# Batch 0 of a pooled attention with gated feed-forward: v pooled in two halves of the heads, with the order and the banks of the first values changed

## The chip, the cores and the metric

The kernel runs on one core of a Trainium2 chip. A core has TensorE (PE, matmuls; PEld is its weight load), VectorE (DVE), ScalarE (ACT), GpSimd (POOL) and SyncE (SP, which here only issues DMAs). Matmuls write to PSUM, eight banks of 512 fp32 columns on 128 partitions. The metric is the device time in microseconds (us) from launch to end.

## The reference

Inputs are q, k, v of shape (8 batches, 8 heads, 576 positions, 64) and two weights, 512x2048 and 2048x512. The output has 4608 rows (8 x 576) of 512.

```
k_p = k.reshape(B, H, 72, 8, 64).mean(axis=3)         # v_p in the same way
scores = q @ k_p^T / 8
attn = softmax(scores)                                # over 72 pooled keys
x = (attn @ v_p), heads side by side                  # 4608 x 512
h = x @ w_in                                          # "up"
out = (h * cos(h)) @ w_out                            # "down"
```

## The kernel before, in words

The 4608 rows of x are held transposed in `xT` and worked off in nine tiles of 512 rows. For each tile t the "up" matmul (`up_mm`, L347) makes h in eight pairs of 128 columns of d_ff, each over four chunks of the contraction (128 rows of `xT` each, two heads); `up_g` (L357) takes the cosine on ACT and multiplies on DVE. Then the "down" matmul makes the output rows, and among its matmuls stands the attention of the next batch. From tile 1 on, down is done in seven products of halved matrices instead of eight.

The order of the work on each engine is the order of the source (`manual_schedule`): each engine works off its instructions in the order in which the code issues them, and waits stand where a tile is read or written. So within PE nothing overtakes.

Ahead of tile 0 stands the attention of batch 0 alone (L533 to L559), since no other work is there to fill the gaps. It is in four units `us[0]` to `us[3]`: units 0 and 1 are heads 0 to 3 at positions 0 to 255 and 256 to 511, units 2 and 3 the same positions of heads 4 to 7. Each unit passes these steps:

- `scores` (L222): eight matmuls or less into a pair of banks, and the exponential on ACT (L240), which leaves `ex`.
- `sums_first` (L306): four matmuls of `ex` with ones (L312), whose logarithm (L316) and exponential of its negative (L317) on ACT give the inverse of the softmax sum. Logarithm and exponential stand in one table of ACT; the sine for up needs another, loaded once by `sin_tables` (L334).
- `values_then` (L320): four matmuls of `ex` with the pooled v (L326) and a DVE multiply by the inverse into `xT` (L328).

Units 0 and 1 fill chunks 0 and 1 of `xT`, units 2 and 3 chunks 2 and 3. So `up_mm(0, 0, 0, 2)` and `up_mm(0, 1, 0, 2)`, the first halves of the contraction of the first two pairs, need units 0 and 1 alone (four matmuls each), and the second halves, which begin tile 0 in the loop (L568), need all four units.

v is pooled on PE by `pool_v_mm` (L181): nine steps, each with a matmul for either half of the partitions (L185), add the groups of eight rows into the two halves of the pair of banks `banks[1]`, 256 columns (four head pairs of 64) in each; one DVE copy (L187) brings all of it to `vz`.

PSUM is three pairs of banks, `banks[0]` to `banks[2]`, and two single banks, `obanks[0]` and `obanks[1]`. The up matmul of tile 0 uses `banks[0]`, `banks[1]`, `banks[2]` in turn. The inverses lie in three buffers in turn (`p1_sb`, `v_sb`, `q_sb`), so that unit 3's takes the buffer of unit 0's.

Batch 0's v is the fourth of the loads on the POOL queue (L490); its landing is what pooling waits for.

Of the kernel before, what the change touches and what calls it, by code (L numbers as in the profile page):

```python
# [20 lines left out]
def kernel(  # L21
# [9 lines left out]
    nc = tc.nc  # L31
    B, H, S, D = q.shape
    Sp = S // POOL
# [4 lines left out]
    KCH = d_model // 128  # L38
# [45 lines left out]
    banks = [psum.tile([128, 2, 512], FP32, name=f"bank{i}") for i in range(3)]  # L84
    obanks = [psum.tile([128, 512], FP32, name=f"obank{i}") for i in range(2)]
# [51 lines left out]
    def v_part(b):  # L137
        return vz[b % 2][:, :, 0:4:3, :]
# [39 lines left out]
                                     start=(t == 0), stop=(t == ROW - 1))  # L178
        return lambda copy: put_kk(b, ps, pj0, pj1, copy)

    def pool_v_mm(b, pair):  # L181
        vb = staged["v", b]
        for t in range(ROW):
            for hp, rows in enumerate(half):
                nc.tensor.matmul(pair[:Sp, hp, 0:KCH * D], lhsT=groups[rows, t, :], rhs=vb[rows, :, t, :],  # L185
                                 start=(t == 0), stop=(t == ROW - 1))
        nc.vector.tensor_copy(out=v_part(b).rearrange("p j a d -> p a j d"),  # L187
                              in_=pair[:Sp, :, 0:KCH * D].rearrange("p a (j d) -> p a j d", j=KCH))

    def k_transpose(b):  # L190
        for i in range(2):
# [25 lines left out]
    def ex_col(u, i):  # L217

        (c0, n), (h0, nh) = u
        return (i // 2 % 2 * (nh // 2) + i // 4 * 2 + i % 2) * n  # L220

    def scores(b, u, pair):  # L222
        scores_mm(b, u, pair)
        scores_exp(b, u, pair)
# [19 lines left out]
    def x_out(b, u, rows):  # L244
        (c0, n), (h0, nh) = u
        return xT[rows, h0 // 2:(h0 + nh) // 2, b * S + c0:b * S + c0 + n]

    def cols(x, u):
        n = u[0][1]
        return x[:, 0:n * u[1][1] // 2].rearrange("p (j n) -> p j n", n=n)  # L250
# [3 lines left out]
    def inverse_tile(w):  # L254

        if early_inverses:
            name = early_inverses.pop(0)
            return msb.tile([128, 2, 256], FP32, name=name, tag=name, bufs=1).rearrange("p a m -> p (a m)")[:, 0:w]
        inv = asb.tile([128, 512], FP32, name="inv", tag="inv", bufs=1)
        return inv[:, 0:w]  # L260
# [45 lines left out]
    def sums_first(b, u, cs):  # L306

        (c0, n), (h0, nh) = u
        ex = att["ex", b, u]
        for i in range(nh):  # L310
            hp = i % 2
            nc.tensor.matmul(cs[hp * 64:hp * 64 + 64, (i // 2) * n:(i // 2 + 1) * n], lhsT=ones[:Sp, :],  # L312
                             rhs=ex[:, ex_col(u, i):ex_col(u, i) + n])
        w = nh * n // 2
        inv = inverse_tile(w)
        nc.scalar.activation(out=inv, in_=cs[:, 0:w], func=ACTF.Ln)  # L316
        nc.scalar.activation(out=inv, in_=inv, func=ACTF.Exp, scale=-1.0)  # L317
        att["inv", b, u] = inv

    def values_then(b, u, ao):  # L320

        (c0, n), (h0, nh) = u
        ex = att.pop(("ex", b, u))
        for i in range(nh):
            pj, hp = divmod(h0 + i, 2)
            nc.tensor.matmul(ao[hp * 64:hp * 64 + 64, (i // 2) * n:(i // 2 + 1) * n],  # L326
                             lhsT=vz[b % 2][:, pj, 3 * hp, :], rhs=ex[:, ex_col(u, i):ex_col(u, i) + n])
        nc.vector.tensor_mul(out=x_out(b, u, slice(0, 128)), in0=cols(ao, u), in1=cols(att.pop(("inv", b, u)), u))  # L328
# [12 lines left out]
    def up_bank(t, fp):  # L341
        i = list(up_order(t)).index(fp)
        if t < FIRST:
            return banks[i % 3]
        return (banks[0], banks[2], banks[1], obanks)[i % 4 if i < 7 else 0]

    def up_mm(t, fp, k0=0, k1=KCH):  # L347

        h = up_bank(t, fp)
        for j in range(2):  # L350
            fc = 2 * fp + j
            for ki in range(k0, k1):
                nc.tensor.matmul(h[j] if h is obanks else h[:, j, :], lhsT=w_in_sb[fc // 4][:, ki, (fc % 4) * 128:(fc % 4 + 1) * 128],  # L353
                                 rhs=xT[:, ki, t * TILE:(t + 1) * TILE],
                                 start=(ki == 0), stop=(ki == KCH - 1))
# [139 lines left out]
    groups = g3.rearrange("p f n -> p (f n)")[:, 0:ROW * Sp].rearrange("p (t n) -> p t n", t=ROW)  # L495
# [34 lines left out]
    us = BY_HEADS  # L530
# [16 lines left out]
    warm_up(2, banks[1][:, 0, :])  # L547
    scores(0, us[2], banks[0])
    scores(0, us[3], banks[2])
    pool_v_mm(0, banks[1])  # L550
    sums_first(0, us[2], obanks[0])
    values_then(0, us[0], obanks[1])
    values_then(0, us[1], banks[1][:, 0, :])
    sums_first(0, us[3], banks[2][:, 0, :])
    values_then(0, us[2], obanks[1])
    values_then(0, us[3], obanks[0])
    up_mm(0, 0, 0, 2)
    up_mm(0, 1, 0, 2)
    sin_tables()  # L559

    for t in range(NT):
        b = t + 1
# [50 lines left out]
        if t == 0:  # L613
            fill = [(2, fill[0][1]), (2, S_(0, 0)), (8, lambda: pool_v_mm(1, banks[1])),
                    (8, lambda: values(t, REST, banks[2])), (8, S_(1, 0)), (8, V_(0, 1)),
                    (18, S_(2, 2)), (21, V_(1, 0, later)), (26, S_(3, 1)), (32, lambda: later.pop()()),
                    (32, V_(2, 2)), (40, V_(3, 0))]
# [132 lines left out]
```

The softmax here doesn't subtract the row's maximum and nothing guards it: scores larger than these inputs give would overflow.

## Time and profile before

| | |
|---|---|
| median of 6 runs | 286.06 us (285.85 to 286.32) |
| the profiled execution | 286.57 us, its span 284.8 us |
| PE | 274.7 us busy, 96% |
| DVE | 215.3 us, 76% |
| ACT | 164.3 us, 58% |
| POOL | 143.3 us, 50% |
| granted TensorE clock | 1.000 over the span |
| v of batch 0 has landed, pooling starts | 12.96 us |
| first up matmul of tile 0 | 16.83 us |

Times within the profile are microseconds from the span's start. A row of the timeline is start, length, engine, line, operation, what is written and read, shape and count; in brackets stands how long the engine had been idle before it and who ended that. A matmul's length is from its start to its modelled end; as matmuls are pipelined, the distance between two starts is what a matmul costs, and rows that stand for several matmuls reach from the first start to the last end. In the chain of work that ended last, each line is a start, a length and a piece of work, and the piece above it is what it waited for.

### The profile page before, as it was taken

The numbers are of one execution on the slowest core, as the hardware profiler recorded it, in microseconds if no ns is written. First come the engines' busy times: TensorE is split into PE (matmuls) and PEld (weight loads), VectorE is DVE, ScalarE is ACT, GpSimd is POOL, SyncE is SP. The second block draws the span as 40 slices with busy tenths as digits, with TensorE's granted clock in tenths as the row PEclk, the third lists the DMA queues.
The fourth block names the chain that finished last, engine by engine and source line by source line (L and its number), as shares of the span: only waits on it lengthen the run. The fifth ranks groups of instructions, "written<-read, shape, count | busy, mean of one in ns | idle before, by whom it ended". The sixth has DMA issues, their size and how long they took to land.

```text
span 284.8 us, 5835 instructions
## 1 busy us (share of the span) xinstructions
PE 274.7 (96%) x2338; PEld 176.4 (62%) x2360; DVE 215.3 (76%) x314; ACT 164.3 (58%) x193; POOL 143.3 (50%) x150
## 2 busy tenths in 40 slices
PE   7889999999999999999999999999999999999994
PEld 2645554446864586458745884588458844874583
DVE  5458747899958995699569956995699569856972
ACT  3886798367157735674566556655656555436600
POOL 8553079996698269924993499439900000000000
PEclk9999999999999999999999999999999999999999
DMA  7999999894949799997778868882660261015014
GB/s 160 199 206 207 207 204 218 124 186 68 137 47 112 148 213 175 139 172 151 111 135 155 175 97 150 147 175 57 123 148 3 55 130 38 0 24 125 2 37 111
DMA packets 57737, 36.12 MB, mean 127 GB/s; under 512 B 35440, under 2 KB 53360, under 8 KB 57712
## 3 DMA queue, kind: packets, MB, share of 16 engines
q0 software_dynamic: 19744, 18.07, 41.4%
q1 hardware_dynamic: 37328, 17.18, 30.9%
q10 hardware_dynamic: 640, 0.52, 0.8%
q8 instruction: 18, 0.29, 0.4%
q14 instruction: 7, 0.06, 0.1%
HBM read 36.70 MB, written 9.44 MB: 162 GB/s over the span
## 4 chain that ended last, share of the span: by engine, by line
PE 78%; DVE 10%; DMA 4%; ACT 3%; issue 1%; SPq 1%; DVEq 0%; ACTq 0%
PE bank L353 33%; PE obank L431 28%; PE obank L370 4%; DVE g_sb L367 4%; PE obank L353 4%; DMA out_dram<-o_two 3%; PE bank L233 3%; DVE g L397 2%; PE bank L431 2%; PE bank L295 2%; ACT cos L363 2%; PE bank L268 1%; SPq L467 1%; DVE w L387 1%; DMA g_sb<-in_k_dram 1%
## 5 line engine op out<-in xcount | busy, mean ns | idle before, releaser
L353 PE MATMUL bank<-xT,w_in_sb 128*128 128x512 bf16 x495 | 113.1, 379 | 1.1 <-DVE g_sb L367 0.2
L363 ACT ACTIVATE cos<-bank,half_pi 128x1024 f32<-128x1024 f32 x64 | 70.3, 1113 | 57.5 <-PE bank L353 55.6
L353 PEld LDWEIGHTS <-w_in_sb 128*128 128x128 bf16 x576 | 56.0, 98 | 66.3 <-issue 0.9
L367 DVE TENSOR_TENSOR g_sb<-bank,cos 128x1024 bf16<-128x1024 f32 x64 | 77.2, 1220 | 25.4 <-ACT cos L363 25.3
L156 POOL TENSOR_TENSOR half_sums<-kv_st 72x512 f32<-72x512 bf16 x48 | 54.7, 1167 | 0.6 <-issue 0.2
L240 ACT ACTIVATE ex<-bank 72x1024 bf16<-72x1024 f32 (+1 forms) x40 | 35.0, 928 | 34.0 <-PE bank L233 33.8
L431 PEld LDWEIGHTS <-g 128*128 128x128 bf16 x512 | 47.8, 98 | 6.2 <-issue 0.3
L431 PE MATMUL obank<-w,g 128*128 128x256 bf16 x368 | 42.7, 273 | 0.2 <-DVE p_sb L445 0.2
L431 PEld LDWEIGHTS <-g_sb 128*128 128x128 bf16 x384 | 36.7, 98 | 7.5 <-issue 0.5
L162 POOL TENSOR_TENSOR half_sums<-half_sums 72x512 f32<-72x512 f32 x24 | 30.4, 1288 | 0.0
L431 PE MATMUL obank<-w_out_sb,g_sb 128*128 128x256 bf16 x240 | 28.9, 273 | 0.0
L397 DVE TENSOR_TENSOR g<-g_sb 128x1024 bf16<-128x1024 bf16 x32 | 23.4, 730 | 0.5
L714 POOL COPY gate<-g 1x1 bf16<-1x1 bf16 x5 | 0.9, 180 | 33.3 <-DVE g L397 33.3
L300 DVE TENSOR_TENSOR x_rows<-bank,inv_rows 128x512 bf16<-128x512 f32 x24 | 16.6, 692 | 0.8
L431 PE MATMUL obank<-w,g_sb 128*128 128x256 bf16 x128 | 15.3, 273 | 0.4 <-DVE o_two L447 0.4
L431 PE MATMUL obank<-w_out_sb,g 128*128 128x256 bf16 x112 | 15.6, 273 | 0.0
L279 DVE TENSOR_TENSOR xT<-bank,inv 64x256 bf16<-64x256 f32 x14 | 5.9, 422 | 12.7 <-ACT inv L275 12.6
L353 PE MATMUL obank<-xT,w_in_sb 128*128 128x512 bf16 x64 | 15.1, 379 | 0.0
L370 PE MATMUL obank<-w_out_sb,g_sb 128*128 128x512 bf16 x61 | 14.7, 380 | 0.4 <-issue 0.3
L233 PE MATMUL bank<-qT,kk 64*72 64x128 bf16 (+2 forms) x288 | 12.6, 222 | 0.1
L233 PEld LDWEIGHTS <-kk 64*72 64x72 bf16 x288 | 9.0, 111 | 5.2 <-issue 3.6
L331 ACT ACT_TABLE_LOAD x9 | 11.5, 1283 | 0.9 <-PEq L734 0.7
(103 smaller groups left out, 276.3 us busy)
## 6 DMA issues: line engine op xcount, KB each, us to landing
out_dram<-o_two SPq DMA_DIRECT2D x64, 128.0 KB, 2.4
kv_st<-in_v_dram POOLq DMA_DIRECT2D x8, 576.0 KB, 11.5
kv_st<-in_k_dram POOLq DMA_DIRECT2D x7, 576.0 KB, 10.0
q_b<-in_q_dram POOLq DMA_DIRECT2D x6, 576.0 KB, 7.5
w_in_sb<-in_moe_w_in_dram POOLq DMA_DIRECT2D x4, 512.0 KB, 13.2
w_out_sb<-in_moe_w_out_dram POOLq DMA_DIRECT2D x4, 512.0 KB, 18.5
q_b<-in_q_dram POOLq DMA_DIRECT2D x4, 288.0 KB, 12.0
g_sb<-in_k_dram SPq DMA_DIRECT2D x1, 576.0 KB, 3.7
```

The costliest lines, as they stand in the source:

```text
L156: nc.gpsimd.tensor_tensor(out=s[:, h:h + 2], in0=x[:, h:h + 2, 0:4, :], in1=x[:, h:h + 2, 4:8, :], op=ADD)
L162: add(out=s[:, h:h + 4, 0:2, :], in0=s[:, h:h + 4, 0:2, :], in1=s[:, h:h + 4, 2:4, :], op=ADD)
L233: nc.tensor.matmul(pair[:Sp, bank, c:c + n].rearrange("p (g n) -> p g n", n=64), lhsT=kk[b % 2][half[r], key_slot(b, h0 + i, r), 0:Sp], rh ...
L240: nc.scalar.activation(out=ex[:, 0:nh * n].rearrange("p (a n) -> p a n", a=2), in_=pair[:Sp, :, 0:nh * n // 2], func=ACTF.Exp, scale=scale ...
L300: nc.vector.tensor_tensor(out=x[0:n].rearrange("p (j a d) -> p j a d", j=KCH, a=2), in0=ps[0:n, :, 0:2 * (D + 2)].rearrange("p j (a w) -> ...
L331: nc.scalar.preload_act_table_set("natural_log_exp_and_others")
L353: nc.tensor.matmul(h[j] if h is obanks else h[:, j, :], lhsT=w_in_sb[fc // 4][:, ki, (fc % 4) * 128:(fc % 4 + 1) * 128], rhs=xT[:, ki, t * ...
L363: nc.scalar.activation(out=c, in_=ps, func=ACTF.Sin, bias=half_pi[:, :1])
L367: nc.vector.tensor_mul(out=o, in0=ps, in1=c)
L370: nc.tensor.matmul(o, lhsT=g_sb[:, fc, ms * 128:(ms + 1) * 128], rhs=w_out_sb[fc // 4][:, fc % 4, :], start=(fc == 0), stop=(fc == FFCH - 1))
L397: nc.vector.tensor_tensor(out=out[:, f0:f1], in0=x, in1=y, op=op)
L431: mms.append(lambda bank=bank, first=first, g=g, w=w, fc=fc, p=p: nc.tensor.matmul(bank[p], lhsT=g(fc, p), rhs=w(fc), start=(first and fc ...
```

## The change

`pool_v_mm` takes a range of head pairs. For batch 0 it is called twice, for head pairs 0 and 1 (heads 0 to 3) and 2 and 3 (heads 4 to 7), each with 18 matmuls of 128 columns and a copy of half the size; both use the same columns of `banks[1]`, so that the second half's matmuls come after the first copy. The values of units 0 and 1 need the first half alone. The order on PE becomes: first half, values of unit 0, second half, values of unit 1, sums of unit 2, values of unit 2, sums of unit 3, the first up matmuls of pair 0, values of unit 3, the first up matmuls of pair 1. The values of unit 1 go to `obanks[0]` instead of `banks[1]`, the sums of unit 2 to `banks[0]` instead of `obanks[0]`. The order on DVE becomes: first copy, multiply of unit 0, second copy, multiplies of units 1, 2 and 3. ACT's order stays. For batch 1 the function is called as before, and no DMA is touched.

```diff
-    def pool_v_mm(b, pair):
+    def pool_v_mm(b, pair, j0=0, j1=KCH):
         vb = staged["v", b]
         for t in range(ROW):
             for hp, rows in enumerate(half):
-                nc.tensor.matmul(pair[:Sp, hp, 0:KCH * D], lhsT=groups[rows, t, :], rhs=vb[rows, :, t, :],
+                nc.tensor.matmul(pair[:Sp, hp, 0:(j1 - j0) * D], lhsT=groups[rows, t, :], rhs=vb[rows, j0:j1, t, :],
                                  start=(t == 0), stop=(t == ROW - 1))
-        nc.vector.tensor_copy(out=v_part(b).rearrange("p j a d -> p a j d"),
-                              in_=pair[:Sp, :, 0:KCH * D].rearrange("p a (j d) -> p a j d", j=KCH))
+        nc.vector.tensor_copy(out=v_part(b)[:, j0:j1].rearrange("p j a d -> p a j d"),
+                              in_=pair[:Sp, :, 0:(j1 - j0) * D].rearrange("p a (j d) -> p a j d", d=D))
...
-    pool_v_mm(0, banks[1])
-    sums_first(0, us[2], obanks[0])
+    pool_v_mm(0, banks[1], 0, 2)
     values_then(0, us[0], obanks[1])
-    values_then(0, us[1], banks[1][:, 0, :])
+    pool_v_mm(0, banks[1], 2, 4)
+    values_then(0, us[1], obanks[0])
+    sums_first(0, us[2], banks[0][:, 0, :])
+    values_then(0, us[2], obanks[1])
     sums_first(0, us[3], banks[2][:, 0, :])
-    values_then(0, us[2], obanks[1])
+    up_mm(0, 0, 0, 2)
     values_then(0, us[3], obanks[0])
-    up_mm(0, 0, 0, 2)
     up_mm(0, 1, 0, 2)
```

## The prediction

> **What bounds the kernel now.** I read the page first: TensorE (PE) is busy 274.7 of 284.8 us at a granted clock of nine tenths or more in every slice, and the chain that ended last is 78% PE. So PE sets the end, and the change can only matter through the moment from which PE runs without a break. That moment lies in the first 20 us. Next I read the chain there, in order of time (start, length, what).
>
> ```profile
> 13.02 1.01 ACT ex L240
> ...
> 14.22 0.70 DVE vz L187
> ...
> 14.96 0.43 PE obank L326 x4
> ...
> 15.49 0.70 DVE xT L328
> ...
> 16.23 0.63 PE obank L326 x8
> 16.86 0.35 PE bank L353
> ...
> 17.26 6.88 PE bank L353 x31
> ```
>
> Seen here: the copy of the pooled v (L187) leads to the first values (L326), one multiply and the other values, and from 16.86 on there is nothing but the up matmul. I read on to the end of this chain: later waits (a DVE stretch from 52 to 60 us, a store before 109.5 us) follow from PE's own progress, and only 0.4 us of PE idling there hangs on a store. So what the first 19 us lose or gain should reach the end nearly whole.
>
> The chain shows what was last, not what was nearly last. The up matmul has a second input gate: its second half of the contraction (k chunks 2 and 3) needs the products of units 2 and 3. Those pass through ScalarE (ACT), whose rows I read from the timeline (start, length).
>
> ```profile
> 14.83 0.59 ACT L316 ACTIVATE q_sb<-obank 128x512 f32<-128x512 f32 x1
> 15.45 0.63 ACT L317 ACTIVATE q_sb<-q_sb 128x512 f32<-128x512 f32 x1
> 16.27 0.60 ACT L316 ACTIVATE p_sb<-bank 128x512 f32<-128x512 f32 x1 [0.20 <-DVE xT L328]
> 16.90 0.63 ACT L317 ACTIVATE p_sb<-p_sb 128x512 f32<-128x512 f32 x1
> 17.55 1.28 ACT L334 ACT_TABLE_LOAD   x1
> ```
>
> Two logarithms (L316) and two exponentials (L317), the inverses of units 2 and 3, end at 17.53. The last multiply follows, on VectorE (DVE):
>
> ```profile
> 14.22 0.69 DVE L187 CAST vz<-bank 72x512 bf16<-72x512 f32 x1 [2.29 <-ACT ex L240]
> ...
> 17.56 0.69 DVE L328 TENSOR_TENSOR xT<-obank,p_sb 128x512 bf16<-128x512 f32 x1
> ```
>
> It ends at 18.25. PE, which began the up matmul at 16.83 at 0.2155 us each (17.47, 17.69, 17.90 in the timeline), comes to the ninth matmul, the first that needs this product, at 16.83 + 8 x 0.2155 = 18.55. With 0.05 us from a DVE end to a PE start (14.91 to 14.96) the gate stands only 18.55 - 18.30 = **0.25 us** from deciding.
>
> **The change, step by step.** Times are us from the span's start.
>
> *Pooling v, first half.* It starts at 12.96 as before, released by the landing of v.
>
> ```profile
> 12.96 1.17 PE L185 MATMUL bank<-kv_st,g 64*72 64x256 bf16 x18 [0.32 <-DMA kv_st<-in_v_dram]
> 14.07 0.41 PE L312 MATMUL obank<-ex,ones 72*64 72x256 bf16 x4
> ```
>
> Eighteen matmuls (nine pairs, the two row halves beside each other) move 128 columns instead of 256. No row has this form. The nearest:
>
> ```profile
> 9.01 0.77 PE L177 MATMUL obank<-g,kv_st 64*64 64x72 bf16 x36
> 10.31 0.45 PE L214 MATMUL bank<-identity,q_b 128*128 128x128 bf16 x5
> ```
>
> The five transposes of 128 columns start 0.056 apart in the trace, the pairs of 72 columns 0.033, the pairs of 256 columns 0.109. I take 0.056, the row with the same columns. It can't be below 0.054, half of the 256-column pace, since half the columns pass; nor does the weight load hold it up much, as the score matmuls with the same 64x72 weights (L233, 64 columns) go at 0.035. I allow up to 0.065. Last start 12.96 + 0.05 + 8 x 0.056 = 13.46, end 0.22 later (a 128-column row's length): **13.67** instead of 14.13.
>
> *First copy.* It starts 0.09 after (14.13 to 14.22). Length by two rows, 144 and 512 columns:
>
> ```profile
> L150 DVE CAST kk<-obank 64x144 bf16<-64x144 f32 x8 | 2.4, 304 | 3.3 <-PE obank L177 3.2
> ```
>
> (686 - 304) / 368 = 1.04 ns a column, so 256 columns take 0.42 (0.34 if all of 0.69 were halved, 0.47 at most, as neighbours with 256 columns are near 0.42). It ends at 13.76 + 0.42 = **14.18** instead of 14.91.
>
> *Values of unit 0* then start at 14.23 (14.96), 0.73 sooner; the second pair of matmuls starts at 14.37.
>
> *Pooling v, second half*, stands behind them on PE. Going over from one shape of matmul to another costs something, seen here:
>
> ```profile
> 35.70 1.17 PE L185 MATMUL bank<-kv_st,g 64*72 64x256 bf16 x18 [0.15 <-DVE g_sb L367]
> 36.80 0.41 PE L268 MATMUL bank<-ex,vz 72*128 72x64 bf16 x8
> ```
>
> The last pair starts at 36.60 in the trace and would let the next go at 36.71; it goes at 36.80, so 0.09 more. The second half starts at 14.37 + 0.20 = 14.57, its last pair at 15.07.
>
> *Values of unit 1* (the first half of v is enough for them) follow over another change of shape at 15.07 + 0.06 + 0.09 = 15.22, second pair 15.35. The second copy on DVE, behind the multiply of unit 0, ends about 15.79; nobody on this path waits for it.
>
> *Sums of unit 2.* This is the step that decides. Before, they ran at 14.07, in the time in which PE waited for the copy. Now they stand behind all of the above: first pair 15.46, second 15.57, end **15.84** instead of 14.48.
>
> *ACT.* It finishes the exponentials of unit 3 at 14.93 as before, and now has nothing until 15.84: about 0.9 us idle where it went straight on. Then, with the lengths of the rows above: logarithm 15.88 to 16.47, exponential 16.50 to 17.13, logarithm of unit 3 from 17.04 (it starts 0.09 before its forerunner's recorded end, as 11.88 against 11.97) to 17.63, exponential 17.66 to **18.29** instead of 17.53. The 0.20 us wait of the 16.27 row goes; that is part of why 1.36 us late at the start is 0.76 late at the end.
>
> *The gate.* Multiply 18.32 to 19.01, PE at 19.06. Its other work is earlier by then: values of unit 2 wait for the second copy (15.85), sums of unit 3 from 16.09, first up matmuls at 16.52 (behind the logarithm of unit 2, which reads their bank), values of unit 3 at 17.48, up matmuls of the second pair from 17.81, free at 18.67. So the 18 added matmuls, the later changes of shape and the new wait in front of the first up weights (0.05; all of PE is queued behind it) lie in 0.39 us of PE waiting. Should they grow by more than that, PE and not ACT is last.
>
> Sum: 19.06 - 18.55 = **+0.51 us**. ACT's table load for the sine ends at 19.59 and the first sine comes at 20.13, so it stays covered. No DMA is moved or made to wait, on SP or POOL.
>
> The bare 0.09 for a change of shape rests on rows. The Trainium skill, TensorEngine Tiling (Array Packing), section Key Properties, says that changing the tiling mode drains TensorE, a rule against this change, which has six such changes for two. If draining meant that the next matmul waits for the recorded end of the last, the two on the path would cost, as an estimate, 0.14 more, and the sum would be +0.65. The row disagrees with so strict a reading: L268 starts at 36.80, before the 36.87 at which L185 ends.
>
> **The rivals.**
>
> *Slower, beyond +0.57.* The same mechanism, ACT waiting for the sums of unit 2, at a dearer price: each 0.01 us on the pace of the two pooled halves costs 0.16, and each change of shape that waits for the last matmul's end 0.07. It decides when the sums of unit 2 end after 15.90. With a pace of 0.065, switches at 0.07 more and a copy of 0.47: 0.51 + 0.14 + 0.14 + 0.05 = +0.84, some 286.9. For it: three prices without a row of their own. Against it: the nearest rows.
>
> *The values' head start counts.* If ACT's gate did not decide, PE would begin the up matmul at 16.52 instead of 16.83 and the end would come 0.3 sooner, 285.8. For it: the copy really is on the chain. Against it: the 0.25 us of slack and ACT's order; it needs the sums of unit 2 to end before 15.1, while copy, values, second half and values must all pass first.
>
> *Swallowed.* The loss is made but given back at the store before 109.5 us, where PE idles 0.4: 286.1. Against it: that store is issued from a queue that follows PE's own results.
>
> **The numbers.** The profiled execution took 286.57 (span 284.8), the median of the six runs is 286.06; I add the sum to each: 287.08 for a profile, **286.57** for the median. A measurement of this kernel can tell about 0.2%, 0.57 us, from no change. Chances: forecast case (+0.2 to +0.57) 0.48, dearer rival 0.42, swallowed 0.05, head start 0.05, of which 0.03 is given to a gain over 0.2%. So faster 0.03, same 0.55, slower 0.42. Low end: pace 0.054, copy 0.34 and free switches take 0.03 + 0.08 + 0.19 off, +0.21, and 0.1 for the spread of runs: 286.2. High end: 286.9 and the upper spread (0.2): 287.1.
>
> **What would show it.** In the new profile: pooled halves of some 0.72 us each; first copy ending near 14.2; ACT idle for about 0.9 us ahead of the logarithm of unit 2, near 15.9; the last multiply of L328 ending near 19.0, and PE waiting for it some 0.4 us after the first up matmuls. I am wrong if that logarithm starts before 15.2, if PE and not DVE is last at the ninth up matmul, or if the delay at 20 us is not found again at the end.

## The result and the profile after

The changed kernel takes 286.74 us in the median of 26 runs; the kernel before, run beside it, 286.15 in 60. The ratio is 1.0018 with a 95% interval of 1.0012 to 1.0024, so a loss of 0.51 us (0.34 to 0.69). The forecast was +0.51 (286.57, counted from a before of 286.06). Here and below a ratio leaves out disturbed executions and a median does not, so that the two need not agree to the last digit.

The chain of work that ended last, in the same stretch as before, now runs through ScalarE (ACT):

```profile
13.87 0.43 DVE vz L187
...
14.34 0.41 PE obank L326 x4
14.75 0.62 PE bank L185 x18
15.37 0.34 PE obank L326 x4
15.71 0.24 PE bank L312 x4
...
15.97 0.61 ACT q_sb L316
...
17.14 0.59 ACT p_sb L316
...
17.75 0.64 ACT p_sb L317
...
18.41 0.70 DVE xT L328
...
19.15 4.94 PE bank L353 x22
```

The copy is shorter, and values of unit 0, second half of v, values of unit 1 and sums of unit 2 follow each other without a gap on TensorE (PE). But then come the two logarithms and exponentials and a multiply, and the up matmul goes on from 19.15. The timelines of ACT and of PE say it from the other side:

```profile
13.03 1.91 ACT L240 ACTIVATE ex<-bank 72x1024 bf16<-72x1024 f32 x2
15.97 0.60 ACT L316 ACTIVATE q_sb<-bank 128x512 f32<-128x512 f32 x1 [1.03 <-PE bank L312]
```

```profile
16.66 1.02 PE L353 MATMUL bank<-xT,w_in_sb 128*128 128x512 bf16 x3
17.61 0.41 PE L326 MATMUL obank<-ex,vz 72*64 72x256 bf16 x4
17.96 1.04 PE L353 MATMUL bank<-xT,w_in_sb 128*128 128x512 bf16 x4
19.15 1.02 PE L353 MATMUL bank<-xT,w_in_sb 128*128 128x512 bf16 x4 [0.16 <-DVE xT L328]
```

ACT is idle for 1.03 us after the exponentials of the scores, until the sums of unit 2 are there; before, it went straight on. PE begins the up matmul 3.58 us after the start of pooling (3.87 before), and then waits for VectorE (DVE) at the ninth. (One record of the first four is missing; the bracket counts idle time from the modelled end of the last matmul.)

The two profiled executions took 286.62 and 286.57 with the same span, though the ninth up matmul comes at 19.15 and 18.55. That is no contradiction, but one execution each: e7 below shows where the difference went.

### The profile page after: what moved, and what is told of

It is laid out like the page before. It is cut to its first block, busy times and chain, and to the rows that moved or that the text cites. A ratio compares the mean times of both kernels' runs of the same rounds, so it can differ in the third digit from the quotient of the medians.

```text
span 284.8 us, 5872 instructions
## 1 busy us (share of the span) xinstructions
PE 275.1 (97%) x2356; PEld 176.3 (62%) x2378; DVE 215.5 (76%) x315; ACT 164.4 (58%) x193; POOL 143.8 (50%) x150
## 4 chain that ended last, share of the span: by engine, by line
PE 85%; DVE 6%; ACT 3%; DMA 2%; issue 1%; POOL 0%; POOLq 0%; DVEq 0%; ACTq 0%
PE bank L353 34%; PE obank L431 32%; PE obank L370 4%; PE obank L353 4%; PE bank L233 3%; DVE g_sb L367 3%; DMA q_b<-in_q_dram 2%; PE bank L295 2%; PE bank L431 2%; PE bank L268 1%; DVE w L387 1%; DVE g L397 1%; ACT cos L363 1%; ACT ex L240 1%; PE bank L185 1%
```

## The experiments

One number is read from every profile: when the ninth up matmul starts, counted from the start of pooling v. Times of the runs scatter by more than the effects looked for; in the twelve profiles pooling starts anywhere between 12.66 and 13.95 us, and whatever hangs on it moves with it. In eleven of them the landing of v releases it; in e6 v had landed at 12.34, and pooling followed the scores on PE. The last column is the profiled execution's time less the ninth up matmul's start.

| kernel | pooling starts | first up | ninth up | ninth less pooling | execution | rest |
|---|---|---|---|---|---|---|
| before | 12.96 | 16.83 | 18.55 | 5.59 | 286.57 | 268.02 |
| after | 13.08 | 16.66 | 19.15 | 6.07 | 286.62 | 267.47 |
| e1 sums of unit 2 early | 13.21 | 16.80 | 19.02 | 5.80 | 286.51 | 267.49 |
| e2 order alone | 12.82 | 16.79 | 19.00 | 6.18 | 286.56 | 267.56 |
| e3 halves alone | 13.51 | 17.27 | 19.00 | 5.49 | 286.50 | 267.50 |
| e4 both sums early | 12.90 | 17.26 | 19.00 | 6.10 | 286.46 | 267.46 |
| e5 values of unit 3 first | 13.49 | 17.32 | 19.56 | 6.07 | 287.04 | 267.48 |
| e6 up first, alone | 12.66 | 16.51 | 18.73 | 6.07 | 286.18 | 267.45 |
| e7 before again | 13.88 | 17.75 | 19.47 | 5.59 | 286.94 | 267.47 |
| e8 both undone | 13.95 | 17.64 | 19.36 | 5.41 | 286.83 | 267.47 |
| e9 after again | 13.22 | 16.80 | 19.30 | 6.07 | 286.74 | 267.44 |
| e10 both undone, v whole | 12.72 | 16.59 | 18.32 | 5.60 | 285.92 | 267.60 |

Eleven of the rests lie within 0.16 us (the twelfth is the first profile of before, see e7): from the ninth up matmul on, all these kernels take the same time, and what is lost or won ahead of it arrives at the end. The distances repeat to a hundredth where a kernel was profiled twice (5.59, 5.59; 6.07, 6.07). The other kernels were profiled once each.

All times in this section lie within 0.5% of before, and the distances tell more than they do. In e1, e2 and e3, which were run together, the ratios say 0.5 to 0.7 us more than the distances do (e1 +0.74 against +0.21, e2 +1.32 against +0.59, e3 +0.57 against -0.10), and the distance lies outside the interval in e2 and e3, at its edge in e1. No trace shows where that comes from, so what these three show rests on their profiles.

**e1: the sums of unit 2 back in the time of the copy.** Against the changed kernel:

```diff
     pool_v_mm(0, banks[1], 0, 2)
+    sums_first(0, us[2], banks[0][:, 0, :])
     values_then(0, us[0], obanks[1])
     pool_v_mm(0, banks[1], 2, 4)
     values_then(0, us[1], obanks[0])
-    sums_first(0, us[2], banks[0][:, 0, :])
```

> The changed kernel with one move: the sums of unit 2 stand right behind the first pooled half, ahead of the values of unit 0, in the time in which TensorE waits for the first copy (13.77 to 14.34 in the changed kernel's profile). Theory 1, that ScalarE is late because the sums of unit 2 come late: its logarithm starts at about 14.85 instead of 15.97, the idle second on ScalarE goes, the last multiply ends near 18.6 instead of 19.10, and TensorE itself, free at about 18.7, decides: 0.4 us faster than the changed kernel, 286.3, some +0.2 against before. Theory 2, that the added matmuls, the second copy and the changes of matmul shape on TensorE cost the time: all of these stay, so the time stays at 286.7.

Measured: 286.61 us, 1.0026 of before (1.0008 to 1.0044); the ninth up matmul 5.80 after the start of pooling, 0.27 sooner than in the changed kernel and not 0.4. By the times e1 is not faster than the changed kernel (1.0018); the 0.27 is the profile's. ACT begins as expected (logarithm of unit 2 at 14.64), but 0.85 us of its idle time only moves, to the logarithm of unit 3, whose sums still come late on PE. Its last exponential ended at 18.00, 4.79 after the start of pooling instead of 5.30, and yet the last multiply begins only at 18.27. The two rows, from ACT's and DVE's timelines of e1, name what each waited for:

```profile
16.74 0.60 ACT L316 ACTIVATE p_sb<-bank 128x512 f32<-128x512 f32 x1 [0.85 <-PE bank L312]
...
18.27 0.69 DVE L328 TENSOR_TENSOR xT<-obank,p_sb 128x512 bf16<-128x512 f32 x1 [0.99 <-PE obank L326]
```

The multiply waits for the values of unit 3 (L326, 17.75 to 18.16 on PE), which stand behind the first four up matmuls. So there is a second holder close behind ACT, and taking ACT's delay away shows it.

**e2: the order without the halves.** Against the kernel before, only the order and the banks of the changed kernel:

```diff
     pool_v_mm(0, banks[1])
-    sums_first(0, us[2], obanks[0])
     values_then(0, us[0], obanks[1])
-    values_then(0, us[1], banks[1][:, 0, :])
-    sums_first(0, us[3], banks[2][:, 0, :])
+    values_then(0, us[1], obanks[0])
+    sums_first(0, us[2], banks[0][:, 0, :])
     values_then(0, us[2], obanks[1])
-    values_then(0, us[3], obanks[0])
+    sums_first(0, us[3], banks[2][:, 0, :])
     up_mm(0, 0, 0, 2)
+    values_then(0, us[3], obanks[0])
     up_mm(0, 1, 0, 2)
```

> The kernel before, v pooled whole in one piece with one copy, but with the changed kernel's order and banks: values of units 0 and 1, then sums of unit 2, values of unit 2, sums of unit 3, first up matmuls, values of unit 3, up matmuls. Theory 1: the sums of unit 2 end at about 15.8 (they wait for the whole copy and the values), the logarithm follows at 15.85, and the ninth up matmul comes at about 19.0: +0.5 against before, 286.65, as with the halves. Theory 2: without the halves there is little to pay: within 0.2 us of before.

Measured: 287.25 us, 1.0046 of before (1.0026 to 1.0067), ninth less pooling 6.18, so 0.59 later than before. By this distance the order alone, without one added matmul, makes the whole loss and a little more. It holds both the late sums of unit 2 and the third part of the change (the first up matmuls ahead of the values of unit 3); e5 and e6 below take these apart. ACT's last exponential ended at 18.12, the values of unit 3 at 18.15: here the two holders are level.

**e3: the halves without the order.** Against the kernel before:

```diff
-    pool_v_mm(0, banks[1])
+    pool_v_mm(0, banks[1], 0, 2)
     sums_first(0, us[2], obanks[0])
+    pool_v_mm(0, banks[1], 2, 4)
```

> v in two halves, all else in the order and banks of before (first half, sums of unit 2, second half behind the first copy, values of unit 0, values of unit 1). Theory 1: the sums of unit 2 keep their place at 14.07 and ScalarE its course; the second half ends near 15.0, the values of unit 0 start near 15.0 as before, the second copy ends near 15.55: the ninth up matmul within 0.1 us of before, time within 0.1 us of before, 286.15. Theory 2: most of the loss, 0.3 us or more.

Measured by the profile: ninth less pooling 5.49, 0.10 sooner than before. Nine up matmuls follow each other from 17.27, and DVE is not late. Measured by the times: 286.67 us, 1.0020 of before (1.0006 to 1.0034), which disagrees. The profiled execution's 286.50 is explained by pooling starting at 13.51, 0.55 later than in the first profile of before; whether that was so in the other executions of these runs no trace shows, so for e3 the mechanism rests on the profile and the times stay open.

**e4: both sums early, values of unit 3 in another bank.** Against the changed kernel the sums of unit 2 move as in e1, the sums of unit 3 stand ahead of the values of unit 2, and:

```diff
-    up_mm(0, 0, 0, 2)
-    values_then(0, us[3], obanks[0])
+    values_then(0, us[3], banks[2][:, 1, :])
+    up_mm(0, 0, 0, 2)
     up_mm(0, 1, 0, 2)
```

> The changed kernel's two halves, with the sums of unit 2 behind the first half, the sums of unit 3 ahead of the values of unit 2, and the values of unit 3 in the free second bank of the third pair, ahead of all up matmuls. Theory 1: the two logarithms and exponentials run through without a long gap (the last exponential ends near 17.3), the last multiply ends near 18.0, the first up matmul at 16.6 is followed by the other seven without a break, and the ninth comes near 18.3, set by TensorE: 0.8 us faster than the changed kernel and 0.25 faster than before, 285.9. Theory 2: the added matmuls and changes of shape are all but one still there: 286.5 or more.

Measured: 286.59 us, 1.0006 of before (0.9979 to 1.0034), ninth less pooling 6.10 instead of 5.2 or so: a miss. ACT ran through from the sums of unit 2 on (15.13 to 17.53) as expected, the last multiply ended at 18.25; PE was late, and its timeline of e4 says why:

```profile
16.92 0.41 PE L326 MATMUL bank<-ex,vz 72*64 72x256 bf16 x4 [0.33 <-ACT p_sb L316]
17.26 1.04 PE L353 MATMUL bank<-xT,w_in_sb 128*128 128x512 bf16 x4
```

By this row the values of unit 3 waited for the logarithm of unit 3 (16.29 to 16.87): it reads the first bank of the third pair, and the program makes a matmul into the second bank of the pair wait for it. A bank that is free by the code was not free by the program's waits. Besides, in this execution the exponential of unit 2's scores ended 1.43 us after the start of pooling (0.95 in the changed kernel's profile), and the values of unit 0 queued behind the sums that waited for it, 0.44 later than in the changed kernel when counted from pooling.

**e5: the third part of the change undone.**

```diff
-    up_mm(0, 0, 0, 2)
     values_then(0, us[3], obanks[0])
+    up_mm(0, 0, 0, 2)
     up_mm(0, 1, 0, 2)
```

> The changed kernel with its third part undone: the values of unit 3 stand ahead of the first up matmuls again. Theory 1: ScalarE's last exponential (18.38) decides and not TensorE, so the time stays within 0.1 us of the changed kernel, 286.7. Theory 2, that TensorE's breaks between matmuls of different shape decide: two changes of shape fewer, 0.2 us faster, 286.5.

Measured: 286.63 us, 1.0010 of the before of that chip (0.9999 to 1.0020); ninth less pooling 6.07, that of the changed kernel. PE has two changes of shape fewer and is done with its first eight up matmuls, and then stands:

```profile
17.32 1.90 PE L353 MATMUL bank<-xT,w_in_sb 128*128 128x512 bf16 x8
19.56 0.38 PE L353 MATMUL bank<-xT,w_in_sb 128*128 128x512 bf16 x1 [0.34 <-DVE xT L328]
```

So PE's breaks are not what holds the changed kernel, and the third part costs nothing there: it lies in time that ACT takes anyway.

**e6: the third part alone**, in the kernel before.

```diff
     values_then(0, us[2], obanks[1])
-    values_then(0, us[3], obanks[0])
     up_mm(0, 0, 0, 2)
+    values_then(0, us[3], obanks[0])
     up_mm(0, 1, 0, 2)
```

> The kernel before with the third part alone: the values of unit 3 behind the first four up matmuls. Here ScalarE is done with unit 3 at 17.53, so the order decides when the last multiply can start: the values of unit 3 start at about 17.8 and end at 18.2, the multiply ends at about 19.0 instead of 18.25 and the ninth up matmul comes at 19.05: +0.5 us, 286.65. If the move only fills TensorE's time, as it is meant: no change.

Measured: 287.28 us, 1.0031 of before (1.0008 to 1.0053); ninth less pooling 6.07, +0.48. The last multiply began at 17.99 and had waited for PE; ACT had ended at 17.41.

```profile
17.99 0.69 DVE L328 TENSOR_TENSOR xT<-obank,p_sb 128x512 bf16<-128x512 f32 x1 [0.86 <-PE obank L326]
```

Where ACT is in time, the third part alone makes a loss of the same size.

**e7: the kernel before, a second profile.**

> The kernel before, unchanged, for a second profile. The first profile of before shows a wait of 0.42 us before 110.27, when a DVE write waits for the buffer of an output store that landed at 109.3; the changed kernel's profile, in which that store landed by 107, has none. If that wait belongs to the one execution, it is gone or different here, and the execution is nearer to 286.1 than to 286.57; if it belongs to the kernel, it is here again.

Measured: one execution of 286.94 us, ninth less pooling 5.59, rest 267.47. The DVE write that stood at 109.53 in the first profile of before is the first line, that of this profile the second:

```profile
109.53 0.69 DVE L447 TENSOR_TENSOR o_two<-obank,q_sb 128x512 f32<-128x512 f32 x1 [3.11 <-PE bank L295]
```

```profile
107.98 0.69 DVE L447 TENSOR_TENSOR o_two<-obank,q_sb 128x512 f32<-128x512 f32 x1 [0.63 <-PE obank L431]
```

The bracket of the first row names a PE instruction. The chain of the same execution shows what was last: an output store that had taken 9.11 us to land (its likes in e7 6.0 to 6.6), and whose buffer the write needs.

```profile
100.20 9.11 DMA out_dram<-o_two
...
109.53 0.70 DVE o_two L447
...
110.27 1.91 PE obank L431 x16
```

The long wait belongs to that one execution, not to the kernel. The four matmuls that start at 109.31 are followed by the next at 110.27, 0.96 later; in e7 the same step, from 110.23 to 110.67, takes 0.44. So it cost PE 0.52 us, nearly all of the 0.55 by which that execution's rest is above the others. But this execution is not nearer to 286.1, as I had expected of it: pooling started at 13.88, 0.92 later than in the first profile of before, and that took the gain back.

**e8: both holders undone, the halves kept.** Against the changed kernel:

```diff
     pool_v_mm(0, banks[1], 0, 2)
+    sums_first(0, us[2], obanks[0])
     values_then(0, us[0], obanks[1])
     pool_v_mm(0, banks[1], 2, 4)
-    values_then(0, us[1], obanks[0])
-    sums_first(0, us[2], banks[0][:, 0, :])
-    values_then(0, us[2], obanks[1])
+    values_then(0, us[1], banks[0][:, 0, :])
     sums_first(0, us[3], banks[2][:, 0, :])
-    up_mm(0, 0, 0, 2)
+    values_then(0, us[2], obanks[1])
     values_then(0, us[3], obanks[0])
+    up_mm(0, 0, 0, 2)
     up_mm(0, 1, 0, 2)
```

> The two halves of v kept, both delays of the last multiply undone: sums of unit 2 behind the first half, values of unit 3 ahead of all up matmuls, and banks in which nobody waits for another (sums of unit 2 and then values of unit 3 in the first single bank, values of unit 1 in the first bank of the first pair). Theory, after e1 and e5: the last multiply of the changed kernel is held by two things of nearly the same date, ScalarE's exponentials (18.38) and the values of unit 3 behind the up matmuls (18.02), so that undoing one gains 0.27 at most or nothing; with both gone TensorE alone decides, the first up matmul starts 3.5 us after the start of pooling (3.58 in the changed kernel, 3.87 before) and the ninth 5.2 us after it (6.07 and 5.59): 0.85 faster than the changed kernel, 0.35 faster than before, 285.8. Rival, that the halves' added matmuls and changes of shape cost: 5.6 or more.

Measured: 286.33 us, 0.9993 of before (0.9974 to 1.0012); ninth less pooling 5.41, 0.66 sooner than the changed kernel and 0.18 sooner than before. The direction holds, the size is half of what I expected against before. PE alone decides: up matmuls follow each other from 17.64 without a wait (one record is missing again, so that the row, cut at 19.7, counts nine where ten ran).

```profile
17.64 2.32 PE L353 MATMUL bank<-xT,w_in_sb 128*128 128x512 bf16 x9
```

What is missing is at the start: the exponential of unit 2's scores ended 1.19 us after the start of pooling, the sums of unit 2 waited for it, and the values of unit 0 came 1.46 after pooling instead of the 1.26 of the changed kernel. By the times e8 is not told apart from before.

**e9: the changed kernel again.**

> The changed kernel once more, for a second profile and a second set of times beside e8 on the same chip. The ninth up matmul 6.07 us after the start of pooling as before, and the time some 0.5 us above the kernel before. If that distance differs by more than 0.1, the sum of my steps held by chance.

Measured: 286.75 us, 1.0013 of before (0.9995 to 1.0031), ninth less pooling 6.07. By the medians that is 0.31 above the before of that chip (286.44); the distance in the profile is the same to a hundredth, that of the times is 0.2 less than expected, within its interval.

**e10: order and banks like e8, v in one piece.**

```diff
     pool_v_mm(0, banks[1])
     sums_first(0, us[2], obanks[0])
     values_then(0, us[0], obanks[1])
-    values_then(0, us[1], banks[1][:, 0, :])
+    values_then(0, us[1], banks[0][:, 0, :])
     sums_first(0, us[3], banks[2][:, 0, :])
-    values_then(0, us[2], obanks[1])
+    values_then(0, us[2], banks[1][:, 0, :])
     values_then(0, us[3], obanks[0])
```

> v pooled whole in one piece as before, with the order of before and banks like those of e8 (values of unit 1 in the first bank of the first pair, values of unit 2 in the first bank of the second pair, so that they needn't wait for the multiply of unit 0). Theory: what the halves bring is an earlier first copy and so earlier multiplies of units 0 and 1; without them the multiply of unit 1 ends at 16.77 as before and the first up matmul starts 3.87 us after the start of pooling, the ninth 5.59: as before, 286.15, 0.35 slower than e8. Rival: the banks and not the halves make e8 faster, then 5.3 or less here too.

Measured: 286.43 us, 0.9993 of before (0.9976 to 1.0009), first up matmul 3.87 and ninth 5.60 after the start of pooling, as before. PE had done the values of unit 3 by 16.01 and then waited for the multiply of unit 1. So by the profiles the banks bring nothing, and the 0.18 of e8 are the halves' own gain, with one execution of each; the times of e8 and e10 (both 0.9993 of before) show no difference.

## Why the prediction was right

Counted from the start of pooling, each step of the sum beside what the changed kernel's profile shows:

| step | predicted | measured |
|---|---|---|
| first half, from start to end | 0.71 | 0.69 |
| first copy | 0.42 | 0.42 |
| values of unit 0 start | 1.27 | 1.26 |
| second half starts | 1.61 | 1.60 |
| values of unit 1 start | 2.26 | 2.22 |
| sums of unit 2 end | 2.88 | 2.85 |
| logarithm of unit 2 starts | 2.92 | 2.89 |
| last exponential ends | 5.33 | 5.30 |
| ninth up matmul | 6.10 | 6.07 |
| against before (5.59) | +0.51 | +0.48 |

**The decisive step**, that the sums of unit 2 lose their place and ACT stands idle, is shown in the profiles by e2 (the order makes the loss without the halves) and by e5 (with the third part undone PE still waits, the multiply for ACT, and the ninth up matmul stays at 6.07); e1 gives the sums their old place and takes 0.51 us off the end of ACT's last exponential. **The dearer rival**, the same wait at a higher price, needed the sums of unit 2 to end after 15.90, 2.94 after the start of pooling; they end at 2.85, and pairs of 128 columns start 0.056 apart, as taken. That the halves as such cost the time is excluded by the profiles of e3 and e8, in which the ninth up matmul comes 0.10 and 0.18 sooner than before; e3's times speak for it, e8's, with the same halves (0.9993), do not. **The change of shape** took 0.20 us after a pair of 256 columns and 0.15 after one of 128, as taken from L268. The stricter reading of the drain in the Trainium skill (TensorEngine Tiling (Array Packing), section Key Properties) would have had the values of unit 1 wait for the end of the second half at 15.37; they start at 15.30, so the trace again shows a pause, but a shorter one.

**The head start** of the values is real (first up matmul 3.58 instead of 3.87 after pooling) and was not decisive, as said. **Swallowed** is what the two first profiles seem to show, 286.57 and 286.62; e7 shows that the store's wait was in that one execution of before, and the medians carry the loss.

Two statements were not good enough, though the sum did not hang on them. The time for a profiled execution, 287.08, was wrong: I added the sum to an execution whose own rest had 0.52 us of store wait that does not recur. I had read that wait as 0.4 us, the idle time from PE's last modelled end; by the distance of the starts it is 0.52, and I should have asked whether the 0.51 by which that execution lay above the median were the same thing. And I took the values of unit 3 behind the up matmuls for well covered "in 0.39 us of PE waiting". The cover of PE's own work was nearly that large (0.32 us: the eighth up matmul starts at 18.61, the ninth at 19.15, where 0.22 is the pace); but the last multiply needs those values, and for it the cover was only the distance from their end (18.02, and 0.11 to a DVE start) to ACT's (18.38, and 0.03), 0.28 us. e1 found it: undoing the main cause alone gives back 0.27 of 0.48.

That the loss by the ratio is +0.51 to the digit is luck: its interval, 0.34 to 0.69, would also hold the lower part of the dearer rival. The firmer agreement is that of the steps, each within 0.04 us, in two executions of the changed kernel.

Open stays why the times of e1, e2 and e3 lie above what their profiles say, and whether e8 is faster than before in the middle of many executions.

## What to carry to other kernels

Work that stands in an engine's waiting time may be there because it feeds another engine's long chain; before it is moved to shorten that wait, follow what it feeds to the next gate and see how much slack that gate has (here 0.25 us). When two things hold the same instruction at nearly the same date, undoing either gives half or nothing (e1 0.27, e5 0 of 0.48), and either alone can cost the full price (e6, and e5 with the halves in); test them together and apart. And where the times scatter with a landing, compare the distance from that landing to the point at which all variants become the same, and check that the rest is constant.

## What the runs showed of the hardware that was not expected

- Pooling of batch 0's v, whose load none of these kernels changes, started between 12.66 and 13.95 us in twelve profiles (v landed between 12.34 and 13.91). That spread of 1.3 us is more than twice the effect of the change, and it reaches the end: the executions whose rests are alike took 285.92 to 287.04 us.
- An output store that landed late at one place (9.11 us after its issue; the DVE write that needs its buffer came at 109.53 against 106.83 to 108.08 in the other eleven profiles) cost PE 0.52 us in one execution of twelve.
